# A position-bias MLP ahead of attention: first layer from one shifted log table on VectorE instead of rank-1 matmuls, and the exponential taken from PSUM

## The chip, the cores and the metric

The kernel runs on one core of one Trainium2 chip. The metric is device time in microseconds (us) from start to end of one execution. Engines: PE is TensorE (PEld its weight loads), DVE is VectorE, ACT is ScalarE, POOL is GpSimd, and SP only issues DMAs.

## The reference

Attention with a learned position bias, then a mixture-of-experts layer with a given expert for each token.

```
B, H, S, D = 8, 8, 576, 64;  hidden = 32;  E = 8 experts, 512 -> 1024 -> 512
scores  = q @ k.T / 8
psi_rel = log1p(|i - j|);  psi_i = log1p(max(i, 1));  x = psi_rel / psi_i      # [S, S]
h       = relu(x * w1 + b1)                                                    # [S, S, 32]
scores += (h @ w2) as one [S, S] matrix for each head
attn    = softmax(scores);  out = attn @ v
for each expert e: rows with domain_id == e:  relu(out @ w1[e]) @ w2[e]
```

The bias depends on no batch, so it is computed once. Softmax takes the exponential of a sum, so the kernel multiplies exp(scores) by exp(bias).

## The kernel before, in words

The program has five phases, written one after the other: constants, bias ("fire"), routing, attention, experts. A scheduling layer orders the instructions of each engine by dependencies and program order, so instructions of a later phase can stand between those of an earlier one where they need nothing from it. Each engine runs its own list in order. Tiles are taken from pools with a number of buffers; a tile whose buffers are all in use makes its writer wait for the last reader. A pool of a later phase takes the memory of one that was closed, and its first writers wait for the last readers there.

Constants. `Tnat` holds x for all i and j, 32 rows of i on 32 partitions in each of 18 blocks. Each block (lines 86 to 100) goes through a POOL iota, DVE casts and absolute value, two ACT logarithms, a DVE reciprocal and a multiplication. `WBIG` holds eight matrices that pick four rows of a block and spread each over 32 hidden units times w1. `Tnat` and `biasall` are set to zero by POOL first (lines 80 and 103). `W2BIG` (128 x 32) holds w2 times 8 for four rows: partition 32g + c is hidden unit c of row g.

Bias. Nine blocks of 64 rows i. In a block, for each of 16 groups of four rows, two matmuls (L119, 512 and 64 columns) bring x * w1 into a PSUM tile `hpre`, 128 partitions (four rows x 32 units) by 576 columns j. DVE adds b1 and takes the relu into `hrelu`, f16 (L126). Then for each of five column chunks j (`JC`: four of 128, one of 64) sixteen small matmuls (L133, `hrelu` as weights, 32 columns of `W2BIG`) give a PSUM tile `eb` with j on partitions and (64 rows i x 8 heads) along it. DVE copies `eb` into `biasall` (L140), which is laid out [j, chunk, head, i], so neighbouring elements of `eb` land 576 elements apart. After all blocks one ACT instruction takes the exponential of `biasall` in place (L141).

Routing. From `domain_id` the kernel works out with small DVE operations (L152 to L196) a slot for each token, `posi`, and writes the token numbers into a table in DRAM, `fire_perm`, with 36 indirect DMAs on POOL (L203), each behind the one before. Its arithmetic is mixed into the bias phase by the scheduler where it can be. One of its steps is a small PE matmul `app` (L172).

Attention. For each of 8 batches: q and k come by POOL DMAs that convert to f16 (L234, L237), v by SP DMAs (L259, L261). For each head PE transposes q and k (L247, L250), DVE copies them to `qkT` (L254, L255), PE makes the scores `sc` (L287), ACT the exponential `eT` (L291), DVE the product with `biasall` (L297). Then PE makes `pu` with v (L308), DVE divides, and SP writes x to DRAM. The first writer of attention's memory is the POOL memset of `qkT` (L231), in memory that the bias phase used.

Experts. For each expert its weights by POOL DMAs, rows of x gathered by indirect DMA (L336), two matmul layers (L348, L356) with relu on ACT (L353) between, DVE copies the result `res` (L359), and an indirect DMA scatters it (L360).

## Time and profile before

| What | Value |
|---|---|
| time, median of 3 runs | 915.02 us (908.75 to 915.71) |
| span of the profiled execution | 900.5 us (its time as a run of its own is not recorded; the median of the runs is 14.5 us above the span) |
| busy share of the span | PE 64%, PEld 42%, DVE 63%, ACT 29%, POOL 32% |
| chain that ended last, by engine | DVE 31%, DMA 24%, PE 20%, issue 10%, ACT 10%, POOL 4% |
| largest lines of that chain | L140 10%, scatter of the results 10%, L291 8%, L126 8% |

The span runs from the first to the last instruction that the hardware profiler recorded. A group row reads: line, engine, operation, output <- input, shapes, xcount, then busy us and the mean ns of one, then the idle time of the engine just before them and what ended it. A row in order of time reads: start us, duration us, engine, line, operation, count, and in brackets how long the engine sat idle before and what ended that. Busy shares are means over phases that have different limits.

### The profile page before, as it was taken

How to read it: one execution, taken by the hardware profiler on the slowest of the kernel's cores; microseconds unless marked ns; L12 is line 12 of the kernel's file. 1: busy time of each engine (PE TensorE's matmuls, PEld its weight loads, DVE VectorE, ACT ScalarE, POOL GpSimd, SP SyncE). 2: the span in 40 equal slices, each digit the busy share in tenths (PEclk: the TensorE clock that was granted, in tenths of full speed). 3: DMA queues.
4: the chain of work that ended last, by engine and by line, in shares of the span. 5: the costliest groups of instructions: out<-in, count | busy, mean ns of one | idle time of the engine just before them, and what ended most of it. 6: DMA issues, size and time to landing. Idle time of an engine off the chain costs nothing.

```text
span 900.5 us, 15948 instructions
## 1 busy us (share of the span) xinstructions
PE 573.2 (64%) x6513; PEld 377.7 (42%) x6513; DVE 570.0 (63%) x1106; ACT 259.0 (29%) x279; POOL 290.8 (32%) x547
## 2 busy tenths in 40 slices
PE   0132555555553387786858778786287977887785
PEld 0011233333332245454536555454265655555563
DVE  5989999999999286766758796886021211121121
ACT  0021200000001973535545383754021211211111
POOL 7821100000001735654523243030343453343451
PEclk9999999999999998969879997999599998999999
DMA  1000000000002968389393949020947647736721
GB/s 3 1 5 1 0 1 1 1 1 0 1 1 28 123 55 74 49 99 72 75 59 76 91 59 104 22 61 25 171 125 153 144 120 159 164 98 149 158 99 60
DMA packets 150233, 60.52 MB, mean 67 GB/s; under 512 B 128656, under 2 KB 141456, under 8 KB 150160
## 3 DMA queue, kind: packets, MB, share of 16 engines
q0 software_dynamic: 93824, 45.12, 38.0%
q1 hardware_dynamic: 56336, 14.39, 7.6%
q8 instruction: 51, 0.84, 0.4%
q14 instruction: 22, 0.18, 0.1%
HBM read 68.35 MB, written 17.34 MB: 95 GB/s over the span
## 4 chain that ended last, share of the span: by engine, by line
DVE 31%; DMA 24%; PE 20%; issue 10%; ACT 10%; POOL 4%; POOLq 0%; SPq 0%; DVEq 0%; ACTq 0%
DVE biasall L140 10%; DMA out_dram<-res,gidx 10%; ACT eT L291 8%; DVE hrelu L126 8%; PE sc L287 5%; PE ops L356 5%; DMA fire_x<-xt 4%; PE hps L348 3%; DMA xg<-fire_x,gidx 3%; DMA fire_perm<-nidx,posi 3%; PE hpre L119 3%; PE pu L308 3%; DVE eT L297 3%; DVE WBIG L77 2%; DMA bm<-in_w_dram 2%
## 5 line engine op out<-in xcount | busy, mean ns | idle before, releaser
L291 ACT ACTIVATE eT<-sc 128x1152 f16<-128x1152 f32 (+1 forms) x192 | 172.3, 965 | 138.3 <-PE sc L287 104.2
L359 DVE COPY res<-ops 128x512 f32<-128x512 f32 x48 | 33.2, 692 | 189.7 <-PE ops L356 127.9
L297 DVE TENSOR_TENSOR eT<-eT,biasall 128x576 f16<-128x576 f16 (+1 forms) x320 | 132.1, 459 | 23.9 <-ACT eT L291 22.5
L119 PE MATMUL hpre<-Tnat,WBIG 128*128 128x512 f16 (+1 forms) x288 | 91.7, 422 | 80.9 <-DVE Tnat L99 40.0
L287 PE MATMUL sc<-qkT 128*128 128x512 f16 (+5 forms) x640 | 117.0, 311 | 36.0 <-DVE qkT L255 17.3
L126 DVE TENSOR_SCALAR hrelu<-hpre,b1x 128x576 f16<-128x576 f32 x144 | 113.6, 818 | 2.4 <-PE hpre L119 2.1
L353 ACT ACTIVATE hsb<-hps 128x1024 f16<-128x1024 f32 x48 | 49.1, 1023 | 223.2 <-PE hps L348 192.6
L356 PE MATMUL ops<-w2e,hsb 128*128 128x512 f16 x384 | 98.5, 403 | 17.7 <-ACT hsb L353 9.5
L133 PE MATMUL eb<-W2BIG,hrelu 128*128 128x32 f16 (+1 forms) x720 | 55.0, 197 | 81.6 <-DVE biasall L140 71.8
L348 PE MATMUL hps<-xgT,w1e 128*128 128x128 f16 x1536 | 101.0, 223 | 6.0 <-DVE xgT L344 5.5
L348 PEld LDWEIGHTS <-w1e 128*128 128x128 f16 x1536 | 95.4, 100 | 21.2 <-issue 11.0
L140 DVE CAST biasall<-eb 128x512 f16<-128x512 f32 (+1 forms) x45 | 104.2, 2595 | 0.0
L308 PE MATMUL pu<-vext,eT 128*128 128x65 f16 (+1 forms) x1600 | 77.8, 211 | 27.1 <-DVE xt L314 18.7
L133 PEld LDWEIGHTS <-hrelu 128*128 128x128 f16 (+1 forms) x720 | 46.3, 126 | 110.2 <-issue 91.2
L360 POOL DMA_INDIRECT out_dram<-res,gidx x48 | 47.4, 988 | 131.3 <-DMA out_dram<-res,gidx 71.5
L308 PEld LDWEIGHTS <-eT 128*128 128x128 f16 (+1 forms) x1600 | 68.4, 112 | 39.4 <-DVE xt L314 26.4
L287 PEld LDWEIGHTS <-qkT 128*128 128x128 f16 (+1 forms) x640 | 51.0, 105 | 66.8 <-issue 23.9
L119 PEld LDWEIGHTS <-WBIG 128*128 128x128 f16 x288 | 28.6, 106 | 109.5 <-issue 55.3
L356 PEld LDWEIGHTS <-hsb 128*128 128x128 f16 x384 | 35.7, 102 | 63.3 <-issue 16.7
L231 POOL MEMSET qkT<- 64x1152 f16 x2 | 2.0, 1052 | 180.8 <-PE eb L133 180.8
L262 POOL CAST vext<-vf 128x256 f16<-128x256 f32 x64 | 29.7, 465 | 80.2 <-PE pu L308 64.2
L336 POOL DMA_INDIRECT xg<-fire_x,gidx x48 | 46.8, 975 | 24.7 <-issue 12.9
(78 smaller groups left out, 612.6 us busy)
## 6 DMA issues: line engine op xcount, KB each, us to landing
vf<-in_v_dram SPq DMA_DIRECT2D x64, 128.0 KB
w1e<-in_moe_w_dram POOLq DMA_DIRECT2D x8, 1024.0 KB
w2e<-in_moe_w_dram POOLq DMA_DIRECT2D x8, 1024.0 KB
q<-in_q_dram POOLq DMA_DIRECT2D x8, 576.0 KB
k<-in_k_dram POOLq DMA_DIRECT2D x8, 576.0 KB
fire_x<-xt SPq DMA_DIRECT2D x32, 128.0 KB
vf<-in_v_dram SPq DMA_DIRECT2D x64, 16.0 KB
xg<-fire_x,gidx POOLq DMA_INDIRECT x48
```

The lines of the kernel that those rows point to most:

```text
L119: nc.tensor.matmul(out=hp[:, js: js + jwd], lhsT=G.WBIG[:, m, :], rhs=G.Tnat[:, blk, js: js + jwd], start=True, stop=True,)
L126: nc.vector.tensor_scalar(out=hr, in0=hp, scalar1=G.b1x4[:], scalar2=0.0, op0=AO.add, op1=AO.max)
L133: nc.tensor.matmul(out=eb[0:jw, 32 * k16: 32 * k16 + 32], lhsT=hrl[k16][:, j0: j0 + jw], rhs=G.W2BIG[:, 0:32], start=True, stop=True,)
L140: nc.vector.tensor_copy(out=oap, in_=eb[0:jw, :])
L287: nc.tensor.matmul(out=po, lhsT=qkT[:, 1, j0: j0 + jw], rhs=qkT[:, 0, i0s: i0s + iwd], start=True, stop=True)
L291: nc.scalar.activation(out=eT[0:jw0, jgl: jgl + njc, :], in_=sc[0:jw0, 0:njc, :], func=AF.Exp, bias=0.0, scale=scale)
L297: nc.vector.tensor_tensor(out=eT[0:jw, jcn, :], in0=eT[0:jw, jcn, :], in1=G.biasall[0:jw, jcn, h, :], op=AO.mult)
L308: nc.tensor.matmul(out=pu[0:icw, hq, 0:65], lhsT=eTs[h][:, jcn, ic0: ic0 + icw], rhs=vexts[h][:, jcn, 0:65], start=(jcn == 0), stop=(jcn = ...
L348: nc.tensor.matmul(out=hps[:, 128 * fc: 128 * fc + 128], lhsT=w1e[:, dc, 128 * fc: 128 * fc + 128], rhs=xgT[:, dc, :], start=(dc == 0), st ...
L353: nc.scalar.activation(out=hsb, in_=hps, func=AF.Relu, bias=0.0, scale=1.0)
L356: nc.tensor.matmul(out=ops_, lhsT=hsb[:, fc, :], rhs=w2e[:, fc, :], start=(fc == 0), stop=(fc == 7))
L360: nc.gpsimd.indirect_dma_start(out=out[:], out_offset=bass.IndirectOffsetOnAxis(ap=G.gidx[:, e, kk: kk + 1], axis=0), in_=res[:], in_offse ...
```

## The change

The first layer no longer goes through PE. A table `L4` (f16, 128 x 1148) holds on the partitions of row g the values log1p(|c - 572 - g|). For the group m of four rows i = 4m + g, the 576 columns of `L4` that begin at 572 - 4m are log1p(|j - i|). So one DVE tensor-scalar multiplies these columns by `slope[:, m]` (w1 over log1p(max(i, 1)), one value a partition) and takes the maximum with -b1. The result is the relu less b1; b1 @ w2 is then missing from the bias as one constant for each head, which softmax does not see. `b1x4`, `bm32`, `WBIG`, `Tnat` and their loads and memsets are gone, as is the memset of `biasall`. `hr` has 40 buffers where `hrelu` had 18. `eb` now takes two banks for two chunks, with four buffers where two of one bank were. ACT takes the exponential straight from `eb`, reading PSUM with a step of eight elements and writing runs of 64 into `biasall`; the DVE copy L140 and the exponential L141 are gone. Lines behind the bias phase move up by 13.

```diff
+NGR = S // 4
+LC = S - 4
+LW = LC + S
...
-    b1col = cst.tile([HID, 1], F32, tag="b1col", name="b1col")
-    nc.sync.dma_start(out=b1col, in_=b1[:].unsqueeze(-1))
-    G.b1x4 = cst.tile([P, 1], F32, tag="b1x4", name="b1x4")
-    for g in range(4):
-        nc.vector.tensor_copy(out=G.b1x4[32 * g: 32 * g + 32, :], in_=b1col)
+    w1col = cst.tile([P, 1], F32, tag="w1col", name="w1col")
+    nc.sync.dma_start(out=w1col, in_=bass.AP(tensor=w1.tensor, offset=0, ap=[[0, 4], [1, 32], [1, 1]]))
+    G.nb1 = cst.tile([P, 1], F32, tag="nb1", name="nb1")
+    nc.sync.dma_start(out=G.nb1, in_=bass.AP(tensor=b1.tensor, offset=0, ap=[[0, 4], [1, 32], [1, 1]]))
+    nc.vector.tensor_scalar(out=G.nb1, in0=G.nb1, scalar1=-1.0, scalar2=None, op0=AO.mult)
...
-    nc.gpsimd.memset(G.WBIG, 0.0)
-    for m in range(8):
...
-    nc.gpsimd.memset(G.Tnat, 0.0)
...
-    for blk in range(18):
...
+    for g in range(4):
+        nc.gpsimd.iota(si[32 * g: 32 * g + 32, :], base=g, channel_multiplier=0, pattern=[[4, NGR]])
+        nc.gpsimd.iota(li[32 * g: 32 * g + 32, :], base=-(LC + g), channel_multiplier=0,
+                       pattern=[[1, LW]])
+    G.slope = cst.tile([P, NGR], F32, tag="slope", name="slope")
+    nc.vector.tensor_copy(out=G.slope, in_=si)
+    nc.vector.tensor_scalar(out=G.slope, in0=G.slope, scalar1=1.0, scalar2=None, op0=AO.max)
+    nc.scalar.activation(out=G.slope, in_=G.slope, func=AF.Ln, bias=1.0, scale=1.0)
+    nc.vector.reciprocal(out=G.slope, in_=G.slope)
+    nc.vector.tensor_scalar(out=G.slope, in0=G.slope, scalar1=w1col[:], scalar2=None, op0=AO.mult)
+    lf = cst.tile([P, LW], F32, tag="lf", name="lf")
+    nc.vector.tensor_copy(out=lf, in_=li)
+    nc.vector.scalar_tensor_tensor(out=lf, in0=lf, scalar=-1.0, in1=lf, op0=AO.mult, op1=AO.max)
+    G.L4 = cst.tile([P, LW], F16, tag="L4", name="L4")
+    nc.scalar.activation(out=G.L4, in_=lf, func=AF.Ln, bias=1.0, scale=1.0)
...
-    nc.gpsimd.memset(G.biasall, 0.0)
...
+        for ib in range(S // 64):
+            hrl = []
+            for k16 in range(16):
+                m = 16 * ib + k16
+                hr = fsb.tile([P, S], F16, tag="hr", name="hr", bufs=40)
+                nc.vector.tensor_scalar(out=hr, in0=G.L4[:, LC - 4 * m: LC - 4 * m + S],
+                                        scalar1=G.slope[:, m: m + 1], scalar2=G.nb1[:],
+                                        op0=AO.mult, op1=AO.max)
+                hrl.append(hr)
+            for jcs in ((0, 1), (2, 3), (4,)):
+                n = len(jcs)
+                jw = JC[jcs[0]][1]
+                eb = fps.tile([P, 2, 512], F32, tag="eb", name="eb", bufs=4)
                 for k16 in range(16):
+                    for lj, jc in enumerate(jcs):
+                        j0 = JC[jc][0]
                         nc.tensor.matmul(
+                            out=eb[0:jw, lj, 32 * k16: 32 * k16 + 32],
                             lhsT=hrl[k16][:, j0: j0 + jw],
                             rhs=G.W2BIG[:, 0:32],
                             start=True, stop=True,
                         )
-                    oap = rap(G.biasall, jc * 8 * S + i0g, [[1, 64], [S, 8]], nparts=jw)
-                    nc.vector.tensor_copy(out=oap, in_=eb[0:jw, :])
-    nc.scalar.activation(out=G.biasall, in_=G.biasall, func=AF.Exp, bias=0.0, scale=0.125)
+                nc.scalar.activation(
+                    out=G.biasall[0:jw, jcs[0]: jcs[0] + n, :, 64 * ib: 64 * ib + 64],
+                    in_=eb[0:jw, 0:n, :].rearrange("p l (i h) -> p l h i", h=8),
+                    func=AF.Exp, bias=0.0, scale=0.125)
```

On DVE, the last two blocks of the bias phase and what follows stand like this before (a row is line, operation, output <- inputs, shape of the output and count):

```order
L126 TENSOR_SCALAR hrelu<-hpre,b1x_68 128x576 x16
L140 CAST biasall<-eb 128x64x8 x4
L140 CAST biasall<-eb 64x64x8
L126 TENSOR_SCALAR hrelu<-hpre,b1x_68 128x576 x15
L181 TENSOR_TENSOR pa<-pb 128x8x36
L140 CAST biasall<-eb 128x64x8 x4
L140 CAST biasall<-eb 64x64x8
L181 TENSOR_TENSOR pb<-pa 128x8x36
L173 COPY apref<-app 128x8
```

Behind the change, the whole DVE list from the setup to the routing reads as follows (`domf`, `eif`, `oh`, `rowtot`, `pa`, `pb` belong to routing, `L_98` is the table `L4`, `nb_68` is -b1):

```order
L139 CAST domf<-dom_1171 128x36
L85 CAST slope<-si 128x144
L86 TENSOR_SCALAR slope<-slope 128x144
L91 CAST lf<-li 128x1148
L143 CAST eif<-ei 128x8
L92 SCALAR_TENSOR_TENSOR lf<-lf 128x1148
L88 RECIPROCAL slope<-slope 128x144
L145 TENSOR_TENSOR oh<-domf,eif 128x288
L89 TENSOR_SCALAR slope<-slope,w1col 128x144
L149 TENSOR_REDUCE rowtot<-oh 128x8
L108 TENSOR_SCALAR hr<-L_98,slope,nb_68 128x576 x144
L151 CAST rowtot_1183<-rowtot 128x8
```

All 144 `hr` now stand in one row with nothing between them, and the rest of the routing arithmetic, which was mixed into the first blocks, comes behind them.

POOL at the start of attention, before:

```order
L231 MEMSET qkT_1941 64x1152
L231 MEMSET qkT_1942 64x1152
L234 DMA q_1945<-in_q_dram 64x72x64
L203 DMA fire_perm<-nidx,posi 6144x1
L237 DMA k_1947<-in_k_dram 64x72x64
L203 DMA fire_perm<-nidx,posi 6144x1
L262 CAST vext<-vf_1972 128x4x64
```

And behind the change:

```order
L218 MEMSET qkT_1276 64x1152
L218 MEMSET qkT_1277 64x1152
L221 DMA q_1280<-in_q_dram 64x72x64
L224 DMA k_1282<-in_k_dram 64x72x64
L190 DMA fire_perm<-nidx,posi 6144x1
L249 CAST vext<-vf_1307 128x4x64
```

The first load of k now stands ahead of the first index scatter, and the second scatter comes later. From there on the lists of all engines are the same as before but for that scatter, one load of v on SP that changes places with its neighbour, the six DVE operations that make `gidx` of the finished index table (L211 to L221, some ten rows later, at the start of the fifth batch, with some `pu` matmuls of the batch before on PE), and the line numbers.

More of the change, by code (lines that the diff above doesn't have):

```diff
@@ L79, in _setup_constants @@
-    G.Tnat = cst.tile([P, 18, S], F16, tag="Tnat", name="Tnat")
-    nc.gpsimd.memset(G.Tnat, 0.0)
-    tmpa = cst.tile([32, S], F32, tag="tmpa", name="tmpa")
-    tmpi = cst.tile([32, S], I32, tag="tmpi", name="tmpi")
-    pcol = cst.tile([32, 1], I32, tag="pcol", name="pcol")
-    pcolf = cst.tile([32, 1], F32, tag="pcolf", name="pcolf")
-    qcol = cst.tile([32, 1], F32, tag="qcol", name="qcol")
-    for blk in range(18):
-        i0 = 32 * blk
-        nc.gpsimd.iota(tmpi, base=i0, channel_multiplier=1, pattern=[[-1, S]])
-        nc.vector.tensor_copy(out=tmpa, in_=tmpi)
-        nc.vector.scalar_tensor_tensor(out=tmpa, in0=tmpa, scalar=-1.0, in1=tmpa,
-                                       op0=AO.mult, op1=AO.max)
-        nc.scalar.activation(out=tmpa, in_=tmpa, func=AF.Ln, bias=1.0, scale=1.0)
-        nc.gpsimd.iota(pcol, base=i0, channel_multiplier=1, pattern=[[0, 1]])
-        nc.vector.tensor_copy(out=pcolf, in_=pcol)
-        nc.vector.tensor_scalar(out=pcolf, in0=pcolf, scalar1=1.0, scalar2=1.0,
-                                op0=AO.max, op1=AO.add)
-        nc.scalar.activation(out=qcol, in_=pcolf, func=AF.Ln, bias=0.0, scale=1.0)
-        nc.vector.reciprocal(out=qcol, in_=qcol)
-        nc.vector.tensor_scalar(out=G.Tnat[0:32, blk, :], in0=tmpa,
-                                scalar1=qcol[:], scalar2=None, op0=AO.mult)
```

34 lines of the change are left out of this document (2 added, 32 removed).

## Prediction

> **What bounds the kernel now.** I first read the stages, with the view that gives the busy time of each engine in stretches of time. Its columns are stretch, length, busy time and (count) of PE, weight loads, DVE, ACT and POOL, then granted clock, DMA share and GB/s.
>
> ```profile
> 0.00:40.00 40.00, 0.00 (x0) 0.00 (x0) 29.96 (x17) 2.06 (x3) 30.84 (x14) 1.00 0.07 2
> 40.00:112.00 72.00, 26.61 (x180) 12.43 (x181) 67.51 (x155) 14.92 (x34) 15.26 (x47) 1.00 0.01 2
> 112.00:285.50 173.50, 96.34 (x829) 53.37 (x828) 173.30 (x152) 0.00 (x0) 0.02 (x1) 1.00 0.00 1
> ```
>
> From 112 to 285.5 us DVE is busy 173.30 of 173.50 us, ACT does nothing, and PE is busy about half the time. The bias stage is a DVE stage. The groups of that stretch say with what:
>
> ```profile
> L140 DVE CAST biasall<-eb 128x512 f16<-128x512 f32 (+1 forms) x39 | 90.0, 2611 | 0.0
> L126 DVE TENSOR_SCALAR hrelu<-hpre,b1x 128x576 f16<-128x576 f32 x112 | 88.0, 822 | 0.3
> L133 PE MATMUL eb<-W2BIG,hrelu 128*128 128x32 f16 (+1 forms) x608 | 45.2, 197 | 66.6 <-DVE biasall L140 65.1 <-DVE hrelu L126 0.6
> ```
>
> Half of it is the scattered copy of `eb` into `biasall` (L140), half the relu out of PSUM (L126). PE's idle time ends on DVE. The first 40 us are a different matter, and the view in order of time shows them:
>
> ```profile
> 7.13 6.93 DVE L152 CAST domf<-dom 128x36 f32<-128x36 int32 x1 [3.40 <-DMA dom<-in_moe_domain_id_dram]
> 17.98 19.67 DVE L89 CAST tmpa<-tmpi 32x576 f32<-32x576 int32 x1
> 17.98 19.29 POOL L103 MEMSET biasall<- 128x23040 f16 x1
> 42.31 0.44 DVE L89 CAST tmpa<-tmpi 32x576 f32<-32x576 int32 x1
> ```
>
> The same cast takes 19.67 us beside POOL's memset of `biasall` and 0.44 us later. DVE stands still until POOL is done, so both large memsets (`Tnat`, `biasall`) are on the path. The first matmul starts at 40.02.
>
> Then the handover to attention, in the same view:
>
> ```profile
> 285.48 2.05 POOL L231 MEMSET qkT<- 64x1152 f16 x2 [180.84 <-PE eb L133]
> 287.48 1.98 POOL L234 DMA_DIRECT2D q<-in_q_dram  x1
> 290.30 19.40 ACT L141 ACTIVATE biasall<-biasall 128x23040 f16<-128x23040 f16 x1
> 294.44 1.04 POOL L203 DMA_INDIRECT fire_perm<-nidx,posi  x1 [4.98 <-DVE posi L196]
> 295.50 1.81 POOL L237 DMA_DIRECT2D k<-in_k_dram  x1
> 303.78 0.69 PE L250 MATMUL ptk<-idn,k 64*64 64x64 f16 x9 [7.31 <-DMA k<-in_k_dram]
> 309.61 2.65 ACT L291 ACTIVATE eT<-sc 128x1152 f16<-128x1152 f32 x3
> ```
>
> POOL's memset of `qkT` waits for the last bias matmul: 285.5 is where attention is let loose. Its first exponential starts 24.1 us later, right behind the 19.40 us exponential over the whole `biasall`. Everything behind hangs on this point, not on an absolute time, and stands in the same order after the change but for one index scatter. So the sum is: when does the changed kernel reach the point of 285.5, and how fast does attention start from there.
>
> **The change, part by part.** *Setup.* Gone are the two memsets, eight w1 loads with their selects, and 18 rounds for `Tnat`. New are eight iotas, five small DVE operations and a logarithm for `slope`, and a cast, an absolute value and a logarithm over 1148 columns for `L4`. Rows for these:
>
> ```profile
> L88 POOL IOTA tmpi<- 32x576 int32 x18 | 10.8, 602 | 38.6 <-DVE pcolf L94 23.6 <-DVE qcol L98 15.1
> L93 POOL IOTA pcol<- 32x1 int32 x18 | 2.1, 119 | 2.2 <-DVE pcolf L94 2.2
> 42.81 0.74 DVE L90 SCALAR_TENSOR_TENSOR tmpa<-tmpa 32x576 f32<-32x576 f32 x1
> L291 ACT ACTIVATE eT<-sc 128x1152 f16<-128x1152 f32 x128 | 137.8, 1127 | 134.8 <-PE sc L287 100.7 <-DVE eT L269 17.1 <-issue 16.9
> ```
>
> An iota is 119 ns + 0.84 ns an element: 1148 give 1.08 us, 144 give 0.24, four of each 5.3 us, so POOL is done near 7 us. Behind its five first small operations DVE has the cast of `dom`, still the fourth load on SP's queue, so it is held to 7.13 as now, but no longer for 6.93 us. From there on DVE: 0.15 for `dom`, 0.4 for two `slope` operations, the cast of 1148 (0.44 for 576, of which 0.14 is fixed: 0.74), `eif` 0.15, the absolute value (0.74 for 576: 1.33), then ACT's logarithm at 1.13, plus some 0.3 for handovers: 11.4. **First hr at 11.5 us**; the rest of `slope` lies beside ACT.
>
> *The new DVE operation, x144.* The trace has no tensor-scalar from f16 in SBUF to f16. The nearest rows:
>
> ```profile
> L188 DVE TENSOR_SCALAR etile<-eif 128x288 f32<-128x288 f32 x1 | 0.3, 291 | 0.0
> 46.16 0.50 DVE L99 TENSOR_SCALAR Tnat<-tmpa,qcol 32x576 f16<-32x576 f32 x1
> 46.58 0.13 DVE L95 TENSOR_SCALAR pcolf<-pcolf 32x1 f32<-32x1 f32 x1
> L297 DVE TENSOR_TENSOR eT<-eT,biasall 128x576 f16<-128x576 f16 x256 | 107.0, 458 | 23.1 <-ACT eT L291 22.0
> L190 DVE TENSOR_TENSOR rtile<-rtile,etile 128x288 f32<-128x288 f32 x1 | 0.5, 458 | 0.0
> ```
>
> A tensor-tensor over 576 f16 costs what one over 288 f32 costs, 458 ns both: the width counts, not the number. Carried over to tensor-scalar, 576 f16 cost the 291 of L188. L99 (0.50) against the cast of the same size (0.44) puts one per-partition operand at 60 ns; hr has two, so 350 to 410 ns. Rows overlap: L95 starts 0.42 behind L99's start, 0.08 before its end. That leaves 0.28 to 0.36 a piece; I take 0.34, near the upper end since two operands are read and buffer waits stand between: 144 x 0.34 = **49 us**. The far bounds are L99 as it stands (0.50, f32 input: 72 us) and L126 (0.79 apart from start to start: 114 us). Below 0.28 nothing here goes.
>
> The Trainium skill, "VectorE: DVE Perf Modes", section "The perf-mode tier table", lets a tensor-scalar on 16-bit SBUF data run at four elements a cycle, and its cost walk-through has some 150 cycles fixed: an estimate of 0.31 us, 45 us in all and an end at 683. L188 with L297 and L190 agrees with that in the part that the rows can show.
>
> *PE.* 288 matmuls L119 go; 720 small ones stay, now five for each hr. What they take unhindered:
>
> ```profile
> 209.26 0.59 PE L133 MATMUL eb<-W2BIG,hrelu 128*128 128x32 f16 x16 [1.71 <-DVE biasall L140]
> 213.82 0.99 PE L133 MATMUL eb<-W2BIG,hrelu 128*64 128x32 f16 x16 [1.69 <-DVE biasall L140]
> 206.80:218.30 11.50, 3.02 (x52) 2.45 (x51) 11.50 (x7) 0.00 (x0) 0.00 (x0) 1.00 0.00 0
> ```
>
> Per block of 64 rows 4 x 0.59 + 0.99 = 3.35 us, against DVE's 16 x 0.34 = 5.4. PE lies beside DVE and leaves about 1 us behind the last hr.
>
> *ACT.* The 45 copies and the 19.40 us exponential go; 27 exponentials straight from PSUM come.
>
> ```profile
> L353 ACT ACTIVATE hsb<-hps 128x1024 f16<-128x1024 f32 x48 | 49.1, 1023 | 223.2 <-PE hps L348 192.6 <-DMA w1e<-in_moe_w_dram 30.6
> L291 ACT ACTIVATE eT<-sc 64x576 f16<-64x576 f32 x64 | 40.9, 639 | 3.5 <-PE sc L287 3.5
> 206.78 11.53 DVE L140 CAST biasall<-eb 128x512 f16<-128x512 f32 x5
> L359 DVE COPY res<-ops 128x512 f32<-128x512 f32 x48 | 33.2, 692 | 189.7 <-PE ops L356 127.9 <-DMA out_dram<-res,gidx 59.7 <-issue 2.1
> ```
>
> At these prices a block is 2 x 1.02 + 0.6 = 2.65 us, hidden under DVE's 5.4. But the new reads take every eighth element of PSUM, and no ACT row does that. L140, which also carries an i/h exchange, takes 11.53/5 = 2.31 us for 512 elements against 0.69 for L359: 3.3 times. There the scattered side is the 2-byte write; now the write runs along 64 neighbours and the read is scattered, so I take the contiguous price (nothing on the path) and keep 3.3 times as the other bound. Cheaper than contiguous would gain nothing, being hidden. New waits: the second and third `eb` of a block wait for ACT to free those of the block before, about 1.3 and 2.4 us into it. Behind them on PE stand the matmuls of the next hr, and DVE would run on, with 40 hr buffers; PE makes up for it at 0.21 us per hr.
>
> *Routing.* On DVE most of the routing arithmetic now stands behind all 144 hr rather than between them: some 18 operations of 0.15 to 0.66 us, about 9 us, beside the 10.3 us that q takes to arrive. The point where attention is let loose is then 11.5 + 49 + 1 = **61.5 instead of 285.5: 224 us less.**
>
> *Start of attention.* The 19.40 us exponential no longer holds ACT. POOL now issues k right behind q, no longer behind the scatter that waited 4.98 us for `posi`. k took 8.3 us from issue to PE; issued 4 us behind the point it is there at 12, scores need 1.5 more, and the first exponential is near 15 instead of 24.1. Late next is POOL's chain of 36 scatters, which starts only some 2.5 us earlier, and DVE waits for its end once, near 452 us:
>
> ```profile
> L211 DVE CAST permEf<-permE 128x48 f32<-128x48 int32 x1 | 0.2, 190 | 6.4 <-DMA permE<-fire_perm 6.4
> ```
>
> That cast comes some ten small rows later now, but the end of the scatters can hold attention there again. So between 2.5 and 9 of this survives; I take **4**, near the chain's own gain. The rest of attention and the expert stage have the same instructions.
>
> Sum: 224 + 4 = 228. The span of 900.5 becomes 672.5. The median of the runs, 915.02, stands 14.5 above that span (I have no separate time for the profiled execution), and I keep that: **687 us**.
>
> **The rivals.** *hr at L99's pace* (f16 input gains nothing): 0.50 each, 23 us more, 710. *hr at L126's pace* (two per-partition operands allow no faster form): 0.79, 65 more, 752. Against both: the 458 pair.
>
> *ACT becomes the bound*: with scattered reads at 3.3 times a block takes 8.7 us on ACT, 78 in all instead of 49, and up to 3.35 a block more where PE refills the freed tiles only then: 716 to 746, some 730 in the middle. For it: L140. Against it: which side is scattered.
>
> *PE becomes the bound at half clock.* PE will be busy only about 60% of the stage. If the clock then fell to half, a block would take 6.7 us, 60 instead of 49: 698. Against it: the stretch 206.80:218.30 above, PE busy 3.02 of 11.50 us at granted clock 1.00. The Trainium skill, "TensorE: Matmul & The Clock Gate", section "What's actually happening", has the clock halve after an idle window of about 3.4 us; by that rule this rival could hold in the gaps of a slow start, and the trace disagrees as far as it goes: the idle stretches there are shorter.
>
> *Slower than before*: if reading columns that shift by four from hr to hr threw DVE into L140's pace, 4.5 ns an element, hr would cost 2.6 us and the stage 374 us: about 1012. It decides from 1.92 us each on ((285.5 + 4 - 12.5)/144). For it only that DVE has such a pace at all; against it, hr's rows are unbroken on both sides.
>
> **How the numbers follow.** Forecast 0.76, with an own range of 670 to 702 (0.28 to 0.41 a piece is -9 and +10 us; the start -5 and +2; runs of this kernel lie 7 us apart). L99's pace 0.08, ACT 0.07, half clock 0.03, L126's pace 0.04, slower 0.02. From 668 to 730 takes in all but L126's pace, the slow case, the upper half of ACT's and the forecast's own tails, somewhat under 2 in 10. A measurement of this kernel tells about 1% from no change; every case but the last is far beyond that: faster 0.97, same 0.01, slower 0.02.
>
> **What would show it.** hr: 144 rows with a mean of 0.35 to 0.41 us, about 0.34 from start to start. First hr at 11 to 12.5. Bias exponentials near 1.0 and 0.6 us; if they read 3 us, the rival holds. Memset of `qkT` at 58 to 65; first attention exponential 12 to 18 us later. Clock 1.00 in between. The stretch from there to the end as long as now, within 10 us; the prediction is wrong if attention grows once it starts with other DMA timing, which no row of before can show.

## The result, and the profile after

The changed kernel takes **685.47 us** (median of four runs, 681.7 to 697.4) against 912.75 us for the kernel before in the same rounds. The ratio is **0.7507, 95% interval 0.7448 to 0.7566**. The forecast was 687 us. It came out that close because its terms were wrong in opposite directions, as shown further down.

The first profiled execution of the changed kernel was a disturbed one (697.4 us, with attention 20 us longer than in the other), so the rows below are from a second profile of the same kernel: span 683.3 us, its own time 685.46 us, from a measurement of its own whose ratio was 0.7559 [0.7483, 0.7635].

First the stages of the changed kernel, in the view by stretches (columns as in the prediction: PE, weight loads, DVE, ACT, POOL, granted clock, DMA share, GB/s):

```profile
0.00:12.50 12.50, 0.00 (x0) 0.00 (x0) 6.79 (x16) 3.35 (x4) 8.54 (x22) 1.00 0.23 5
12.50:61.50 49.00, 42.33 (x635) 35.32 (x635) 49.00 (x147) 17.56 (x22) 0.00 (x0) 1.00 0.01 2
61.50:68.30 6.80, 5.82 (x87) 4.89 (x87) 0.85 (x4) 2.69 (x4) 0.00 (x0) 1.00 0.00 0
```

The setup ends at 12.5 us instead of 40. The 144 `hr` take 49.00 us, and DVE is busy in all of it. Then comes a piece that the prediction gave 1 us: for 6.8 us DVE has almost nothing to do and PE goes on alone. (The clock of 1.00 in these rows is not a measurement: this trace has no clock record before 87.7 us, and the view counts full clock where there is none. More on that further down.) The groups up to 75 us, with the row of the profile's page that takes both shapes of L119 together, say with what:

```profile
L108 DVE TENSOR_SCALAR hr<-L,slope,nb 128x576 f16<-128x576 f16 x144 | 49.0, 423 | 0.0
L119 PE MATMUL eb<-W2BIG,hr 128*128 128x32 f16 x576 | 35.5, 191 | 17.9 <-DVE hr L108 12.9 <-ACT biasall L125 4.9
L119 PE MATMUL eb<-W2BIG,hr 128*64 128x32 f16 x144 | 26.3, 228 | 2.2 <-ACT biasall L125 2.2
L119 PE MATMUL eb<-W2BIG,hr 128*128 128x32 f16 (+1 forms) x720 | 48.1, 199 | 20.1 <-DVE hr L108 12.9
L125 ACT ACTIVATE biasall<-eb 128x1024 f16<-128x1024 f32 x18 | 17.4, 1021 | 35.6 <-PE eb L119 35.6
L125 ACT ACTIVATE biasall<-eb 64x512 f16<-64x512 f32 x9 | 5.2, 583 | 0.0
```

DVE's `hr` never waits (0.0 behind the last bar). The exponential from strided PSUM costs 1021 and 583 ns, the price of contiguous reads. PE is what runs over: its 144 matmuls with 64-column weights show 26.3 us, three quarters of what the 576 with 128 columns do. The two shapes overlap in time, so these don't add up: together they keep PE busy for 48.1 us. In order of time, from the setup to the first exponential of attention:

```profile
5.10 0.15 DVE L67 TENSOR_SCALAR nb<-nb 128x1 f32<-128x1 f32 x1 [5.10 <-DMA nb<-in_b_dram]
5.36 1.71 DVE L73 TENSOR_SCALAR W2BIG<-w2sb 32x8 f16<-32x8 f32 x4
7.50 0.18 DVE L139 CAST domf<-dom 128x36 f32<-128x36 int32 x1 [0.43 <-DMA dom<-in_moe_domain_id_dram]
10.62 1.04 DVE L88 RECIPROCAL slope<-slope 128x144 f32<-128x144 f32 x1
56.84 0.64 PE L119 MATMUL eb<-W2BIG,hr 128*128 128x32 f16 x18 [0.62 <-ACT biasall L125]
62.97 0.64 PE L119 MATMUL eb<-W2BIG,hr 128*128 128x32 f16 x18 [0.62 <-ACT biasall L125]
63.88 4.32 PE L119 MATMUL eb<-W2BIG,hr 128*64 128x32 f16 x56 [0.27 <-ACT biasall L125]
68.32 2.05 POOL L218 MEMSET qkT<- 64x1152 f16 x2 [58.94 <-PE eb L119]
72.27 1.80 POOL L224 DMA_DIRECT2D k<-in_k_dram  x1
82.91 0.69 PE L237 MATMUL ptk<-idn,k 64*64 64x64 f16 x9 [3.56 <-DMA k<-in_k_dram]
85.38 2.73 ACT L278 ACTIVATE eT<-sc 128x1152 f16<-128x1152 f32 x3 [14.95 <-PE sc L274]
```

The cast of `dom` takes 0.18 us where it took 6.93 beside the memset. A block of 64 rows repeats on PE every 62.97 - 56.84 = 6.13 us, of which 0.62 + 0.27 are waits for ACT, while DVE makes one in 16 x 0.340 = 5.44. The handover (memset of `qkT`) is at 68.3, and the first exponential of attention 17.1 us behind it.

### The profile page after: what moved, and what is told of

Same layout as the page of the kernel before. It is cut to its first block, busy times and chain, and to the rows that moved or that the text cites. A ratio compares the mean times of both kernels' runs of the same rounds, so it can differ in the third digit from the quotient of the medians.

```text
span 695.2 us, 15154 instructions
## 1 busy us (share of the span) xinstructions
PE 527.6 (76%) x6225; PEld 361.6 (52%) x6225; DVE 357.3 (51%) x948; ACT 250.6 (36%) x271; POOL 252.5 (36%) x508
## 3 DMA queue, kind: packets, MB, share of 16 engines
q1 hardware_dynamic: 55400, 14.25, 10.6%
## 4 chain that ended last, share of the span: by engine, by line
PE 39%; DMA 24%; ACT 12%; DVE 9%; issue 9%; POOL 5%; POOLq 0%; SPq 0%; ACTq 0%; DVEq 0%
PE sc L274 10%; PE ops L343 9%; DMA out_dram<-res,gidx 8%; ACT eT L278 6%; PE eb L119 6%; PE hps L335 5%; DMA fire_x<-xt 4%; PE pu L295 4%; ACT hsb L340 4%; DVE eT L284 4%; DMA fire_perm<-nidx,posi 3%; DMA xg<-fire_x,gidx 3%; ACT biasall L125 2%; DMA w1e<-in_moe_w_dram 2%; PE ptk L237 2%
## 5 line engine op out<-in xcount | busy, mean ns | idle before, releaser
L278 ACT ACTIVATE eT<-sc 128x1152 f16<-128x1152 f32 (+1 forms) x192 | 175.7, 966 | 176.7 <-PE sc L274 174.3
L274 PE MATMUL sc<-qkT 128*128 128x512 f16 (+5 forms) x640 | 141.7, 359 | 23.6 <-DVE qkT L242 14.7
L346 DVE COPY res<-ops 128x512 f32<-128x512 f32 x48 | 33.2, 692 | 179.8 <-PE ops L343 111.2
L295 PEld LDWEIGHTS <-eT 128*128 128x128 f16 (+1 forms) x1600 | 68.3, 112 | 50.5 <-DVE xt L301 24.3
L274 PEld LDWEIGHTS <-qkT 128*128 128x128 f16 (+1 forms) x640 | 53.5, 115 | 64.5 <-issue 29.4
L119 PE MATMUL eb<-W2BIG,hr 128*128 128x32 f16 (+1 forms) x720 | 48.1, 199 | 20.0 <-DVE hr L108 12.9
L190 POOL DMA_INDIRECT fire_perm<-nidx,posi x36 | 39.6, 1101 | 47.1 <-DMA fire_perm<-nidx,posi 39.4
L234 PE MATMUL ptq<-idn,q 64*64 64x64 f16 x576 | 44.2, 216 | 14.4 <-DMA q<-in_q_dram 8.5
L234 PEld LDWEIGHTS <-q 64*64 64x64 f16 x576 | 33.1, 127 | 41.5 <-issue 30.6
L119 PEld LDWEIGHTS <-hr 128*128 128x128 f16 (+1 forms) x720 | 40.1, 112 | 27.9 <-DVE hr L108 12.9
L328 PE MATMUL pxt<-idn,xg 128*128 128x128 f16 x192 | 17.8, 240 | 43.3 <-DMA xg<-fire_x,gidx 43.2
L108 DVE TENSOR_SCALAR hr<-L,slope,nb 128x576 f16<-128x576 f16 x144 | 49.0, 442 | 0.0
```

Source lines behind the costliest of these rows:

```text
L108: nc.vector.tensor_scalar(out=hr, in0=G.L4[:, LC - 4 * m: LC - 4 * m + S], scalar1=G.slope[:, m: m + 1], scalar2=G.nb1[:], op0=AO.mult, op ...
L119: nc.tensor.matmul(out=eb[0:jw, lj, 32 * k16: 32 * k16 + 32], lhsT=hrl[k16][:, j0: j0 + jw], rhs=G.W2BIG[:, 0:32], start=True, stop=True,)
L234: nc.tensor.transpose(out=ptq[:, 64 * m: 64 * m + 64], in_=q16[0:64, g9, :], identity=G.idn[0:64, 0:64])
L274: nc.tensor.matmul(out=po, lhsT=qkT[:, 1, j0: j0 + jw], rhs=qkT[:, 0, i0s: i0s + iwd], start=True, stop=True)
L278: nc.scalar.activation(out=eT[0:jw0, jgl: jgl + njc, :], in_=sc[0:jw0, 0:njc, :], func=AF.Exp, bias=0.0, scale=scale)
L295: nc.tensor.matmul(out=pu[0:icw, hq, 0:65], lhsT=eTs[h][:, jcn, ic0: ic0 + icw], rhs=vexts[h][:, jcn, 0:65], start=(jcn == 0), stop=(jcn = ...
```

## The experiments

What is read from each profile is the handover (the start of the memset of `qkT`), the stretch from there to the issue of the last write of x (attention), and the time from the handover to the end of the span. All in us; for runs with several times the median and the ratio to the kernel before, with its interval, stand beside them; a single time is one run.

| run | handover | attention | handover to end | span | time, ratio |
|---|---|---|---|---|---|
| before | 285.5 | 336.2 | 615.0 | 900.5 | 912.75 |
| a0 (the changed kernel) | 68.3 | 335.5 | 615.0 | 683.3 | 687.30, 0.7559 [0.7483, 0.7635] |
| a1 | 62.0 | 338.4 | 614.9 | 676.9 | 681.18, 0.7466 [0.7370, 0.7561] |
| a2 | 63.2 | 341.0 | 618.1 | 681.3 | 683.70 |
| a4 | 53.3 | 348.4 | 626.8 | 680.1 | 682.29 |
| b1 | 179.8 | 346.9 | 626.1 | 805.9 | 807.64 |
| b2 | 195.8 | 336.9 | 616.7 | 812.5 | 814.19 |
| b3 | 267.4 | 360.8 | 643.2 | 910.6 | 912.46 |
| c1 | 64.8 | 335.8 | 614.6 | 679.4 | 675.68, 0.7396 [0.7342, 0.7450] |
| d2 | 62.0 | 338.1 | 615.7 | 677.7 | 682.96, 0.7475 [0.7414, 0.7535] |
| e2 | 64.8 | 335.2 | 613.8 | 678.6 | 680.24, 0.7441 [0.7381, 0.7500] |
| f1 | 64.8 | 338.7 | 614.7 | 679.5 | 681.95, 0.7521 [0.7457, 0.7585] |
| f3 | 65.3 | 334.7 | 602.2 | 667.5 | 669.25 (routing left out, so only attention is to be read) |

**Why PE runs over: the width of the weights (a0, a1, a2, a4).** Theory: PE pays for each change between weights of 128 columns and of 64, and the scheduler lets the five chunks of an `hr` follow one another, so it changes twice for each. Rival: PE waits for ACT to free `eb`. a0 is the changed kernel again, without an edit.

> The changed kernel unaltered, beside the variants on one chip. Both theories: the memset of qkT (the handover) near 68 us, DVE done with hr near 61, blocks of 6.1 us. Time 680 to 690.

In a1 the fifth chunk also takes 128 columns, the last 128, and ACT reads the upper half of the result. No matmul has 64-column weights then; the number of matmuls, the `eb` tiles and ACT's work stay as they were.

```diff
-                        j0 = JC[jc][0]
+                        j0 = min(JC[jc][0], S - P)
...
-                            out=eb[0:jw, lj, 32 * k16: 32 * k16 + 32],
-                            lhsT=hrl[k16][:, j0: j0 + jw],
+                            out=eb[:, lj, 32 * k16: 32 * k16 + 32],
+                            lhsT=hrl[k16][:, j0: j0 + P],
...
-                    in_=eb[0:jw, 0:n, :].rearrange("p l (i h) -> p l h i", h=8),
+                    in_=eb[P - jw: P, 0:n, :].rearrange("p l (i h) -> p l h i", h=8),
```

> The last column chunk loads 128 weight columns (448 to 575) instead of 64; the exponential reads the upper half of the result. DVE and ACT do the same work. Theory 'width change': PE loses time each time it goes between 128-wide and 64-wide weights, twice in each group of five; without it a group takes 5 x 27 = 135 ns instead of 386, PE waits for DVE again, and the handover comes at 12.4 + 49 + 1 to 2 = 62 to 64, 4 to 6 us earlier. Rival 'eb buffers': PE is late because it waits for ACT to free eb, twice in each block; then nothing changes and the handover stays at 67 to 69.

In a2 the 64-column chunk stays, but the sixteen of a block come together, one block late (`tiles` holds the matmuls and the exponential as they were):

```diff
+        def tiles(ib, hrl, jcs):
...
+            tiles(ib, hrl, (0, 1))
+            if late is not None:
+                tiles(ib - 1, late, (4,))
+            tiles(ib, hrl, (2, 3))
+            late = hrl
+        tiles(S // 64 - 1, late, (4,))
```

> The same matmuls as the changed kernel, but the 64-wide ones of a block stand together behind the next block's first ones: 4 changes of width a block instead of 32. Theory 'width change': a block on PE takes about 64 x 27 + 16 x 53 ns + 4 x 0.15 us = 3.2 us, DVE sets the pace, handover at 62 to 65. Rival 'eb buffers': the tiles' waits stay, handover 67 to 70. If 64-wide matmuls were dear in themselves, also 67 to 70.

The groups of a1 (first row) and a2 (second, its 64-column matmuls alone), and the handover of each, a1 first:

```profile
L119 PE MATMUL eb<-W2BIG,hr 128*128 128x32 f16 x720 | 44.0, 191 | 17.9 <-DVE hr L108 12.9
```

```profile
L110 PE MATMUL eb<-W2BIG,hr 128*64 128x32 f16 x144 | 12.6, 218 | 0.0
```

```profile
61.98 2.05 POOL L218 MEMSET qkT<- 64x1152 f16 x2 [52.60 <-DVE etile L175]
```

```profile
63.20 2.05 POOL L226 MEMSET qkT<- 64x1152 f16 x2 [54.49 <-PE eb L110]
```

Twice as wide a weight makes PE *faster*: 720 matmuls keep it busy 44.0 us instead of 48.1, and the handover comes 6.3 us earlier, half a microsecond behind the last `hr`. The 64-column matmuls kept together show 12.6 us instead of 26.3, and the handover is at 63.2. So it isn't the 64 columns as such but the changing. PE's 16 waits for ACT to free `eb`, 7.1 us in a0, are gone in a1 and a2, though the tiles are the same: they come with PE's lateness. They do add to it, though, once it is there: without them a block of a0 would take 5.24 us, just under DVE's 5.44, and no run takes them away alone. The single records of a0's last block, where DVE is done, give the price: starts lie 26 to 27 ns apart between 128-column weights, 117 to 118 ns on the way to the 64-column one and 168 to 170 back, with one more gap of 46 to 48 ns behind that.

In a4, a1 loses its second operand: b1 is left out of `hr`.

```diff
-                                        scalar1=G.slope[:, m: m + 1], scalar2=G.nb1[:],
+                                        scalar1=G.slope[:, m: m + 1], scalar2=0.0,
```

> As the variant with 128 wide weights in all chunks, and hr takes the maximum with the constant 0 instead of -b1 (b1 is left out of the computation). Shows the price of the second per-partition operand and whether DVE now sets the pace. Theory 'width change': hr's mean falls from 0.44 by 0.06 to 0.08 us and its pace from 0.340 by as much, to 0.27 to 0.28; the handover follows by 144 times that, to 53 to 56. Rival 'eb buffers': handover stays at 67 to 69 whatever DVE does.

Its group and its handover:

```profile
L108 DVE TENSOR_SCALAR hr<-L,slope 128x576 f16<-128x576 f16 x144 | 40.3, 364 | 0.0
```

```profile
53.27 2.05 POOL L218 MEMSET qkT<- 64x1152 f16 x2 [43.87 <-DVE etile L175]
```

(49.0 - 40.3)/144 = 0.060 us: that is a per-partition operand, as the prediction took it from L99 and L89. The handover moves by the same 8.7 us, so in a1 it is DVE that sets it. Once PE doesn't change weights it does a block in under a4's 16 x 0.280 = 4.5 us.

**What each half of the change is worth alone (b1, b2, b3).** b1 has the new first layer with the old way out: a copy of each `eb` on DVE, one exponential at the end, and the memset of `biasall` that this needs.

```diff
+    nc.gpsimd.memset(G.biasall, 0.0)
...
-                nc.scalar.activation(
-                    out=G.biasall[0:jw, jcs[0]: jcs[0] + n, :, 64 * ib: 64 * ib + 64],
...
+                oap = rap(G.biasall, jc * 8 * S + 64 * ib, [[1, 64], [S, 8]], nparts=jw)
+                nc.vector.tensor_copy(out=oap, in_=eb[0:jw, :])
+    nc.scalar.activation(out=G.biasall, in_=G.biasall, func=AF.Exp, bias=0.0, scale=0.125)
```

> Only the first half of the change: hr from the shifted table, but eb copied by DVE and one exponential over biasall at the end, biasall set to zero by POOL as before. DVE: 16 x 0.34 + 11.5 = 17 us a block, 153 in all, behind POOL's memset of 19.3 us that holds DVE until 27: handover near 180, first exponential 24 behind it, span near 795. If the copies L140 were slow only because PE wrote beside them, they would be faster now and the handover nearer 140.

b2 is the reverse: the kernel before, with rank-1 matmuls and relu, but exponentials straight from `eb`; its two large memsets stay.

```diff
+                for jcs in ((0, 1), (2, 3), (4,)):
...
-                    oap = rap(G.biasall, jc * 8 * S + i0g, [[1, 64], [S, 8]], nparts=jw)
-                    nc.vector.tensor_copy(out=oap, in_=eb[0:jw, :])
+                    nc.scalar.activation(
+                        out=G.biasall[0:jw, jcs[0]: jcs[0] + n, :, i0g: i0g + 64],
+                        in_=eb[0:jw, 0:n, :].rearrange("p l (i h) -> p l h i", h=8),
+                        func=AF.Exp, bias=0.0, scale=0.125)
-    nc.scalar.activation(out=G.biasall, in_=G.biasall, func=AF.Exp, bias=0.0, scale=0.125)
```

> Only the second half of the change: Tnat, WBIG and the matmuls L119 stay, the exponential is taken from PSUM. DVE loses 45 copies of 2.31 us: 104 us less, a block is 16 x 0.79 = 12.6 us, handover near 180; the exponential of 19.4 us goes as well. Span near 795 to 800. If the scattered PSUM reads were dear (3 us instead of 1.02), ACT would still hide under 12.6 us. ACT's tables of logarithm and exponential alternate eight times at 1.28 us, hidden likewise.

b3 is the kernel before with the memset of `biasall` cut to the part that nothing else writes:

```diff
-    nc.gpsimd.memset(G.biasall, 0.0)
+    nc.gpsimd.memset(G.biasall[64:P, NJC - 1], 0.0)
```

> The kernel before, and POOL sets only the 64 partitions of biasall to zero that the copies never write (a fifth of the columns). If DVE's 19.67 us cast is POOL's memset, it becomes 4 us, the first matmul comes near 25 instead of 40, the handover near 270, and the span is 15 us less. Rival: those 20 us are covered by something else (the loads of w1), then less than 5.

Rows of b1, of b2 and of b3, a fence each (b1's memset and copies, b2's relu and handover, b3's memset and handover):

```profile
6.69 19.30 POOL L97 MEMSET biasall<- 128x23040 f16 x1
L123 DVE CAST biasall<-eb 128x512 f16<-128x512 f32 x36 | 83.7, 2598 | 0.0
179.79 2.05 POOL L214 MEMSET qkT<- 64x1152 f16 x2 [151.89 <-PE eb L116]
```

```profile
L126 DVE TENSOR_SCALAR hrelu<-hpre,b1x 128x576 f16<-128x576 f32 x144 | 109.2, 808 | 6.5 <-PE hpre L119 5.5
195.81 2.05 POOL L236 MEMSET qkT<- 64x1152 f16 x2 [94.14 <-PE eb L137]
```

```profile
18.11 4.19 POOL L103 MEMSET biasall<- 64x4608 f16 x1
267.41 2.05 POOL L231 MEMSET qkT<- 64x1152 f16 x2 [180.81 <-PE eb L133]
```

The first layer alone moves the handover by 285.5 - 179.8 = 105.7 us, the exponential alone by 89.7. Together they move it 217.2, which is 21.8 more than the sum; the memset of `biasall`, still in both and worth 18.1 in b3, covers most of that. The copies of b1 take 2598 ns, as in the kernel before (2611): they are as slow without the matmuls L119 and the relus from PSUM beside them, which leaves their own pattern. b2's handover was expected near 180 and came 16 later. Most of that is idle time: between 40 us and the handover DVE sits idle for 15.2 of 155.8 us, against 4.7 of 245.5 in the kernel before, and it waits for PE (`hpre`), for ACT and POOL in the rounds of the setup that stay in this kernel. The time that the copies left there isn't all saved. b3's handover is 18.1 earlier, but its one time of 912.46 stands beside 908.71 for the kernel before: the end didn't come earlier in this run, as its attention took 360.8.

**Where the earlier start goes (c1, d2, e2, f1, f3).** From the handover to the end the profiles of before and a0 both need 615.0 us, although attention's first exponential comes 17.1 us behind the handover instead of 24.1. The prediction said that POOL's chain of scatters would hold back part of it. The rivals: DVE's wait for the end of that chain, POOL's casts of v, or something that sits in attention itself.

c1 makes the start much earlier: on top of a1, q and k get memory of their own, so their loads can start in the setup and not behind the last bias matmul.

```diff
-            q16 = asb.tile([D, 72, D], F16, tag="qk16", name="q16", bufs=4)
+            q16 = G.qkp.tile([D, 72, D], F16, tag="qk16", name="q16", bufs=4)
-            k16 = asb.tile([D, 72, D], F16, tag="qk16", name="k16", bufs=4)
+            k16 = G.qkp.tile([D, 72, D], F16, tag="qk16", name="k16", bufs=4)
+    G.qkp = ctx.enter_context(tc.tile_pool(name="qkp", bufs=1))
```

> As the variant with 128-wide weights, and the tiles of q and k lie in memory of their own, so that POOL issues the loads of the first two batches at the start of the bias stage and not behind it. Theory 'scatter chain': the first attention exponential comes about 6 us behind the handover instead of 18, but the index table is complete (cast of permE) at the same 228 to 240 us, and the end is the same within 4 us. Rival 'the start passes through': the end comes 10 to 13 us earlier than without it.

d2 moves DVE's wait: on top of a1, the reading of the scatter table (`permE` and the five operations behind it) goes from the routing phase into the expert phase.

```diff
-    permE = pbuf.tile([P, E * NCH, 1], I32, tag="permE", name="permE")
...
+    G.perm_dram = perm_dram
...
+        permE = msb.tile([P, E * NCH, 1], I32, tag="permE", name="permE")
```

> As the variant with 128-wide weights, and the load of the finished index table with the six DVE operations behind it stands at the start of the expert phase, so DVE does not wait for the end of the 36 scatters in the fifth batch. Theory 'scatter chain holds attention through DVE's wait': 2 to 10 us less. Rival 'it holds attention through POOL, where scatters stand between the casts of v': the same within 3 us.

e2 has both edits, c1's and d2's.

> Both of the two changes above together. 'Scatter chain through DVE's wait': the earlier start of attention now passes through, 10 to 15 us less than the variant with 128-wide weights alone. 'Through POOL': 0 to 5 us less.

In order of time in c1, and one row of d2 in the second fence:

```profile
8.68 2.06 POOL L221 DMA_DIRECT2D q<-in_q_dram  x1
64.82 2.05 POOL L218 MEMSET qkT<- 64x1152 f16 x2 [45.11 <-PE eb L119]
71.39 2.15 ACT L278 ACTIVATE eT<-sc 128x1152 f16<-128x1152 f32 x2 [4.19 <-PE sc L274]
228.44 0.19 DVE L198 CAST permEf<-permE 128x48 f32<-128x48 int32 x1 [13.90 <-DMA permE<-fire_perm]
```

```profile
418.21 0.19 DVE L305 CAST permEf<-permE 128x48 f32<-128x48 int32 x1 [18.16 <-DMA permE<-fire_perm]
```

c1's first exponential comes 6.6 us behind the handover, 14.0 us earlier in the program than a0's, and still 614.6 us pass from the handover to the end in this profile. DVE then waits 13.9 us for the scatter table, which looks like the held-back gain; but e2 has no such wait in the middle of attention and needs 613.8, and d2 gains nothing either, with its wait now at the start of the experts.

f1 is c1 with the casts of v on DVE, f3 is c1 with a single scatter instead of 36:

```diff
-                nc.gpsimd.tensor_copy(out=vext[:, 0:4, 0:D], in_=vf[:, 0:4, :])
-                nc.gpsimd.tensor_copy(out=vext[0:64, 4, 0:D], in_=vf[0:64, 4, :])
+                nc.vector.tensor_copy(out=vext[:, 0:4, 0:D], in_=vf[:, 0:4, :])
+                nc.vector.tensor_copy(out=vext[0:64, 4, 0:D], in_=vf[0:64, 4, :])
```

> As the variant with 128-wide weights and early loads of q and k, and the two casts of v to vext run on DVE instead of POOL. Theory 'scatters hold attention through the casts of v that stand behind them on POOL': attention from the handover to the last write of x falls from 336 us to 315 to 325, the time by as much, 655 to 668. Rival 'through the loads of q and k behind them, or the DMA engines': 336 within 6, time 670 to 680; with DVE as the next bound it could even grow.

```diff
-    for c in range(36):
+    for c in range(1):
```

> As the variant with 128-wide weights and early loads of q and k, but only one of the 36 index scatters is issued and the table is set to fixed valid numbers (the routing is left out, so only the time up to the end of attention is to be read). Theory 'scatter chain': eight batches at 37 us each behind an early start give 300 to 310 us from the handover to the last write of x, instead of 336. Rival 'the scatters cost nothing': 330 to 340.

Attention took 338.7 in f1 and 334.7 in f3. Without the scatter chain, with POOL busy some two thirds as long, and with a start 6.6 us behind the handover, attention lasts in these profiles as long as in that of the kernel before, where it starts 24.1 behind. So neither the chain nor DVE's wait for it shows as what holds it. POOL's casts don't either, though f1 gives DVE some 15 us more work (259.9 us busy in 336 against c1's 244.5), which could hide a gain. The same 336 us from the handover on in the stretches of three kernels, and a row of the scores each, in the order before, a0, f3:

```profile
285.50:621.50 336.00, 240.55 (x3253) 165.37 (x3252) 242.98 (x673) 192.89 (x194) 136.25 (x374) 0.89 0.74 70
L287 PE MATMUL sc<-qkT 128*128 128x512 f16 (+5 forms) x640 | 117.0, 311 | 36.0 <-DVE qkT L255 17.3
```

```profile
68.30:404.30 336.00, 260.72 (x3270) 172.14 (x3270) 243.78 (x675) 176.34 (x195) 136.12 (x374) 0.81 0.81 70
L274 PE MATMUL sc<-qkT 128*128 128x512 f16 (+5 forms) x640 | 131.9, 340 | 27.0 <-DVE qkT L242 15.3
```

```profile
65.30:401.30 336.00, 266.58 (x3393) 175.37 (x3392) 247.25 (x691) 176.85 (x195) 89.02 (x335) 0.82 0.71 65
L274 PE MATMUL sc<-qkT 128*128 128x512 f16 (+5 forms) x640 | 136.3, 350 | 30.7 <-DVE qkT L242 18.8 <-ACT eT L278 7.8 <-POOL vext L249 1.9
```

From before to a0 PE is busy 20 us more for about the same number of records (3253 and 3270). The clocks of 0.89 and 0.81 count the stretch up to the first clock record (318.9 and 87.7 us) as full; at half, which the durations there show (next section), they are 0.84 and 0.78, and busy time by clock is 203 and 204. The DVE column hardly moves. ACT's is 16.6 less, most of the 19.4 us exponential. So between these two profiles what attention gains at its start goes with slower matmuls. Within one profile, two neighbouring stretches of a1 show the tie of clock and progress:

```profile
188.00:230.00 42.00, 35.48 (x357) 21.99 (x357) 25.64 (x75) 18.94 (x21) 19.40 (x50) 0.57 0.80 71
230.00:272.00 42.00, 33.06 (x473) 22.76 (x472) 34.43 (x100) 24.57 (x28) 14.56 (x43) 0.91 0.90 89
```

At 0.57 granted, PE is busier and gets through 357 matmuls; at 0.91 through 473. This is an association and not a cause that was switched on and off. What sets the granted clock **stays open**.

**How far two profiles carry this.** b3 has the attention of the kernel before, instruction for instruction, and needs 24.6 us more for it than the profile of before, at a clock of 0.75 by the same count; a4's 348.4 go with 0.76. So a difference of some us between two single profiles says little, and the profile of before is a quick one: its span of 900.5 is below that of all 22 other executions of that kernel whose span is on record (900.9 to 927.7). Those other spans help. If the handover is where the profile has it in every execution (68.2 and 68.3 in the two of the changed kernel, 64.8 in c1, e2 and f1), the median time from handover to end is, as an estimate, 624 us in the kernel before (the 18 executions of these that the ratios rest on) and 615 in the changed kernel (7). The profile of b1 agrees: it still has the long exponential, its clock in attention is 0.79 beside a0's 0.78, and it needs 626.1 where a0 needs 615.0. **By these estimates some 9 to 11 us behind the handover were gained, and the two profiles hide it.** Whether c1's further 10 us pass through stays open: by the same count a1 has 615, c1 609, e2 613, f1 615 and d2 618, and c1's profile is that of the longest of its four runs.

**The best version** by its median is c1: its interval [0.7342, 0.7450] lies below that of a0, [0.7483, 0.7635], and touches that of the first measurement of the same kernel, [0.7448, 0.7566]. It overlaps those of a1, d2 and e2, so which of these is best isn't settled. All of them have the 128-column weights; that these alone shorten the whole time isn't settled by the intervals of a1 and a0 either, only that they bring the handover forward.

## Why the prediction was right, and where it wasn't

**The pace of `hr`: right, with some luck.** 144 rows take 49.00 us as predicted, 0.340 each, and a4 confirms the price of an operand that the sum used. The mean of one row, 423 ns, is above the 350 to 410 foretold, while the overlap of 0.08 us is as read. Taken from 350 to 410 that overlap leaves 0.27 to 0.33 and not the 0.28 to 0.36 that the prediction wrote; 0.34 lay above its own rows, as the measured row does.

**The exponential from PSUM: right.** 1021 and 583 ns against 1.02 and 0.6. The rival by which scattered reads cost 3.3 times falls, as do those of slower paces for `hr`. What is left as slow in L140 is the scattered 2-byte write on DVE; no run writes that way on ACT or reads scattered on DVE.

**Clock in the bias stage: misread.** The prediction took 1.00 from the views, but the first clock record of the kernel before is at 318.9 us, and without one the view counts full clock. The durations tell. L119 with 512 columns takes 584 ns in the bias stage of before (first row). b2 has the same matmul and records from 117 us on: 377 ns in a stretch at 1.00, 582 in one at 0.50.

```profile
L119 PE MATMUL hpre<-Tnat,WBIG 128*128 128x512 f16 x110 | 64.2, 584 | 10.5 <-DVE hrelu L126 3.0
```

```profile
131.20:158.00 26.80, 19.24 (x250) 11.72 (x250) 26.39 (x36) 6.05 (x8) 0.00 (x0) 1.00 0.00 1
L119 PE MATMUL hpre<-Tnat,WBIG 128*128 128x512 f16 x36 | 13.6, 377 | 5.7 <-DVE hrelu L126 5.6
```

```profile
168.60:175.10 6.50, 6.17 (x60) 3.37 (x59) 5.73 (x8) 2.53 (x3) 0.00 (x0) 0.50 0.00 0
L119 PE MATMUL hpre<-Tnat,WBIG 128*128 128x512 f16 x8 | 4.7, 582 | 0.3
```

So the bias stage of before ran at half clock, and a0's goes by the same sign: its transposes of q ahead of the first record take 239 ns each, between 88 and 111 us at 1.00 they take 196, and its L119 rows with 128 columns take 191 on average, where b2's same matmul (L137) takes 193 in the stretch at 0.50 and 177 in that at 1.00. The rival "PE becomes the bound at half clock" thus had its condition met all along. Its price was wrong, since the 3.35 us a block that it doubled were measured at half clock already; that PE became a bound, and a block took 6.13 beside its 6.7, comes from the changes of width. What they cost at full clock no run shows.

**First `hr` at 11.5: 1.0 short.** DVE is no longer held behind the load of `dom`, as said. But that load lands at 7.50 and not at 7.13; the second operation on `slope` (L86) takes 0.86 us beside a POOL memset, where b1 shows 0.24; and the reciprocal (1.04) with three more rows stands on DVE for 1.8 us where ACT's logarithm beside it takes 1.16.

**PE hidden with 1 us left over: mis-sized, 5.9 of the 10.8 us.** The step "PE makes up for it at 0.21 us per hr" took its price from bursts of one kind of weight. In the order in which the scheduler puts them, one `hr` costs PE 6.13/16 = 0.383 us, more than DVE's 0.340, so PE is a second bound and falls behind block by block. The difference lies in the changes of weight width: a1 and a2 are without most or all of them and keep up with DVE. (Without its waits for ACT one `hr` would cost a0 0.328.) By the Trainium skill, "TensorE: Matmul & The Clock Gate", section "Weight-path perf modes — Fast Weight Load (FWL) and DoubleRow", the fast load is on where the number of weights is 128 and the type isn't FP32. That agrees with the 26 to 27 ns between 128-column weights against 53 to 54 ns between 64-column ones where those come in a run (sixteen in 0.99 us in the kernel before), both at half clock; the page has no price for going from one to the other, which here is most of it.

**Start of attention, 4 us kept: 0 between the two profiles, some 9 by the runs.** The start itself came 17.1 behind the handover instead of the 15 foretold; k needs 10.6 us from issue to PE (8.3 before), which I put down to q and k loading at once. By the runs, then, the whole gain of 7 us at the start is kept and the term was too small; the profile of before doesn't show that because its execution was a quick one. That "POOL's chain of 36 scatters" is late next doesn't show in f3, a single run.

**From span to time: 14.5 us added, 2.2 measured.** I took the gap between the one profiled span before and the median of other runs for a fixed cost. It isn't one: a0's own time is 685.46 at a span of 683.3. In the runs of the kernel before the gap is 1.7 to 1.9, so its profiled execution took some 902.3, below all its timed runs (902.65 to 929.49). The span came out at 683.3 and not 672.5, 10.8 late (1.0 + 5.9 + 4.0 within rounding); this error of 12.3 the other way all but cancels it. A forecast of the span alone would have been 1.6% off, not 0.2%. Told by medians it is the same cancelling: the fall of 227.3 us (912.75 to 685.47) against the 228 of the sum is 217.2 at the handover instead of 224, and some 10 behind it instead of 4. The mechanism held in the main; that the number is this close is luck.

## What to carry to other kernels

Price small matmuls in the order in which they are issued, not from bursts of one shape: mixing 64- and 128-column weights can cost more than computing the 64 unused columns. Before reading a few us out of one profile of each kernel, see how far the same instructions spread from execution to execution: here attention took 336.2 and 360.8 us, and the gain of some 9 us stands only in the spans of many runs. Look where the clock records of a trace begin; before that, durations of a known shape tell the clock and the column doesn't. And take the step from span to run time from the same execution, or leave it out.

## What the runs showed of the hardware that I had not expected

- A change of weight width on PE delays the next matmul to 117 to 118 ns on the way to 64 columns and 168 to 170 ns back, against 26 to 27 ns without one (matmuls of 32 columns in a0's bias stage, at half clock by its durations).
- POOL's issue of converting loads holds DVE. In the stretch in which c1 issues q and k, DVE gets through 14 `hr`, in a0 through 23 (c1 first; the columns are DVE, clock, DMA share and GB/s of L108 alone):

```profile
12.50:20.00 7.50, 7.16 (x14) 1.00 3.62 142
```

```profile
12.50:20.00 7.50, 7.50 (x23) 1.00 0.00 0
```

  It isn't a slower pace. One `hr` stands there for 1.59 us, to just behind the end of the issue beside it:

```profile
12.52 1.78 POOL L221 DMA_DIRECT2D q<-in_q_dram  x1
12.84 1.59 DVE L108 TENSOR_SCALAR hr<-L,slope,nb 128x576 f16<-128x576 f16 x1
```

  Another takes 1.73 beside the issue of k at 17.83, and those between keep their 0.34 from start to start while the data arrive. With a first `hr` 0.38 later that is where c1's handover loses its 2.8 us against a1's.
- The granted clock was 0.57 to 1.00 in stretches of 42 us of attention, and by the durations half in the bias stage, behind 12.9 us in which PE did nothing. The Trainium skill, "TensorE: Matmul & The Clock Gate", section "What's actually happening", has half clock as the default and behind an idle window of about 3.4 us, and full clock behind a busy one as long. The half clock after the idle setup agrees with that. But the bias stage stayed at half clock with PE busy 42.33 of 49.00 us, and in a1 the clock is 0.50 in a stretch in which PE is busy 25.14 of 25.40; there the trace doesn't agree, and no run here shows what decides.

```profile
204.60:230.00 25.40, 25.14 (x181) 13.08 (x179) 16.70 (x46) 18.44 (x20) 12.72 (x28) 0.50 0.30 37
```
